# Gated two-branch mixer: skip and spectral rows summed by ScalarE and an accumulating DMA, back rotation finished by an accumulating DMA, new pacing of the two streams

## Chip, cores and metric

One core of a Trainium2 chip (trn2) runs the kernel. The metric is device time in microseconds (us) from the start of the launch to its end. A profiled execution is also cut into a trace, whose span runs from the first to the last instruction.

## The reference

The input `x` has 2048 rows of 1024 values. Two branches are computed from it and mixed row by row:

```
g   = sigmoid(sum(x * gate_w, -1))                      # one gate per row
a   = irfft2(rfft2(x) * (w_r + i w_i))                  # spectral branch
Lb  = exp(dt * Lambda);  Bb = ((Lb - 1) / Lambda) * B   # state-space branch
h_t = Lb * h_(t-1) + Bb @ x_t                           # 1024 complex states
b_t = 2 * Re(C @ h_t) + x_t * Dskip
out = g * a + (1 - g) * b
```

`x * Dskip` is called the skip part here, and `g * a` the gated spectral part. Inputs and output are bf16.

## The kernel before

The work has two streams that share all engines, and an output stage.

**The spectral stream** (`fstage`, then `fft_main`) does the 2-D transform as matrix products: `fstage` folds and transforms along one part of the rows, `fd`, `bf_w` and `bi` (16 groups `g`) do the column transform, the product with the filter and the first inverse step, and `idm` and `fi` (16 indices `j`) the rest. The result `ya` goes to a scratch array in DRAM (L576), 256 KB for each of 16 writes, and is read back by row tiles later.

**The state-space stream** (`ssm_all`) handles the recurrence in 4 chunks `c` of 512 time steps and 4 quarters `q` of the states, 16 blocks in all. Each block has a part on TensorE, `ssm_pe`: 4 groups of 8 matmuls `psu` (L388), and after each group one ScalarE copy with a scale into the tile `u` (L390). The tile `u` has two buffers, and the PSUM tile of a group has two as well. The part on VectorE, `ssm_dve`, rotates the states so that the recurrence becomes real (three operations, L399, L401, L403), scans (L408, four instructions), keeps the carry for the next chunk (L417 to L421), and rotates back: two products (L425, L427) and their sum `h` (L429). `h` is in bf16, 128 partitions of 2 x 2 x 512. The rotation tables of a quarter are made by `tables` in chunk 0. For chunk 1 the tile `h` lies in `big`, for chunk 2 in `xT`, and for chunks 0 and 3 in four tiles of their own.

**The output stage** (from L726) works on 16 row tiles `tb` of 128 rows. A tile belongs to chunk `tb // 4` and has two halves of 512 columns. `half(tb, dh)` runs 16 matmuls `psy` of 512 columns (L770), which read all four `h` tiles of the chunk, two matmuls for each of 8 state blocks. For `tb < 11` the skip part is added by one more matmul, the row tile `xc` (multiplied by `Dskip` on VectorE, L758) with an identity matrix (L774). VectorE then leaves PSUM with one operation (L779): `psy * (1 - g) + gac`, where ScalarE has multiplied the spectral row tile `gac` by the gate (L760). For `tb >= 11` the skip part is taken into an fp32 row tile `xf` by ScalarE (L763) and VectorE (L764) instead. The PSUM tile `psy` has three buffers.

**What sets the order.** The functions are Python generators. `ssm_all` and `fft_main` count their own estimated time `t`, and a loop (L717 to L720) takes the next step from the state-space stream while its `t` lies below a line in the other's `t`: 20 by the spectral stream's 54.4, then to 42 over the next 35. Steps then run up to 43 (L792), and a second loop (L796 to L800) interleaves the rest with the halves of the output stage, with the factor 1.02. A scheduler orders the instructions of an engine from this program order, with its own estimates. SyncE (SP, which issues most DMAs) and GpSimd (POOL) keep the written order up to L748 (`order1`); after that the scheduler orders them too. Semaphores between engines follow from the tiles. The final order of every engine is fixed when the kernel is built.

Of the kernel before, what the change touches and what calls it, by code (L numbers as in the profile page):

```python
# [20 lines left out]
D = 1024  # L21
K = 512
P = 128
# [113 lines left out]
def kernel(  # L137
# [213 lines left out]
    def tables(q):  # L351
        xa = rp.tile([P, 2 * TC], FP32, name="xa", tag="cu")
        for jj in range(2):
            jb = 2 * q + jj
            xj = xa[:, TC * jj:TC * (jj + 1)]
            if q < 2:
                nc.vector.tensor_scalar(out=xj, in0=tau_f, scalar1=thp[:, jb:jb + 1], scalar2=beta[:, jb:jb + 1],
                                        op0=ALU.mult, op1=ALU.add)
            else:
                nc.scalar.activation(out=xj, in_=tau_f, func=ACT.Identity, scale=thp[:, jb:jb + 1],  # L360
                                     bias=beta[:, jb:jb + 1])
        rr, ra = frac(xa, 2 * TC, "xa", rp, "su")
        tq = tab[:, 2 * q:2 * q + 2]
        rr = rr.rearrange("p (a t) -> p a t", a=2)
        ra = ra.rearrange("p (a t) -> p a t", a=2)
        nc.scalar.activation(out=tq[:, :, 0, :], in_=ra, func=ACT.Sin, scale=-TWO_PI_LO, bias=chpi)
        nc.scalar.activation(out=tq[:, :, 1, :], in_=rr, func=ACT.Sin, scale=-TWO_PI_LO)
        nc.vector.tensor_scalar_mul(out=tq[:, :, 2, :], in0=tq[:, :, 1, :], scalar1=-1.0)

# [24 lines left out]
    def ssm_dve(c, q, u):  # L394
# [29 lines left out]
        h = h_tile(c, q)  # L424
        nc.vector.tensor_mul(out=cu, in0=su, in1=tq[:, :, 0:1, ::-1].to_broadcast(full))  # L425
# [4 lines left out]
        hs[c, q] = h  # L430
# [65 lines left out]
    def bf_w(g):  # L496
# [17 lines left out]
        (nc.vector.tensor_copy if g < 3 else nc.scalar.copy)(out=X[:, :, 1:513:2], in_=po)  # L514
# [88 lines left out]
    def fft_main():  # L603
# [24 lines left out]
        for jj in range(9):  # L628
            if jj < 8:
# [8 lines left out]
                if jj == 4:  # L638
                    gt = gates()
                    next(gt)  # L640
                    yield 2.0
                if jj == 4 + 1:
                    next(gt)
                    yield 0.3
# [37 lines left out]
    def ssm_all():  # L682
        prev = iter(())
        for c in range(NCH):
            for q in range(4):
                if c == 0:
                    tables(q)
# [29 lines left out]
    while not fft.done:  # L717
        if ssm.t < (20 * (fft.t - 3.5) / (54.4 - 3.5) if fft.t < 54.4 else 20 + (42 - 20) * (fft.t - 54.4) / 35.0):
            ssm.step()
        else:  # L720
            fft.step()
# [4 lines left out]
    with ExitStack() as bctx:  # L726
# [7 lines left out]
        def load_xc(tb):  # L734
            xcs[tb] = fin.tile([P, D], BF16, name="xc", bufs=3)
            nc.sync.dma_start(out=xcs[tb], in_=x[P * tb:P * (tb + 1), :])

        def load_gac(tb):
            gacs[tb] = fin.tile([P, D], BF16, name="gac", bufs=4)
            nc.sync.dma_start(out=gacs[tb], in_=ya_dram[P * tb:P * (tb + 1), :])  # L740

        for tb in range(3):
            load_xc(tb)
        load_gac(0)
        load_gac(1)
        load_C(1)
        load_gac(2)
        order1.close()  # L748

        psys = {}  # L750

        def half(tb, dh):
# [3 lines left out]
            psy, xc, gac = psys[tb], xcs[tb], gacs[tb]  # L756
            if dh == 0:
                nc.vector.tensor_mul(out=xc, in0=xc, in1=dsk_bc)  # L758
            else:
# [71 lines left out]
```

## Time and profile before

| | us |
|---|---|
| median of 13 runs | 354.85 |
| lowest, highest | 353.06, 358.51 |
| the profiled execution | 358.51 |
| its span in the trace | 356.7 |
| TensorE (PE) busy in the span | 330.8 |
| VectorE (DVE) busy | 302.6 |
| ScalarE (ACT) busy | 178.2 |
| GpSimd (POOL) busy | 28.7 |

The profiled execution is the slowest of the 13. Some 1.8 us of its time lie outside of the span. Its TensorE clock was granted at 0.989 of full speed over the span. The spectral stream ends at about 165 us of the span (the last `ya` write is issued at 165.8 us), and the first `psy` matmul starts at 165.82 us. The busy time of an engine says how full it is, not whether the end waits for it; the chain that ended last and the list of waits are needed for that. A matmul in the trace lasts longer (379 ns) than the distance to the next one, since matmuls overlap.

### The profile page before, as it was taken

Reading aid. Unit: us, or ns where it says so; the run is one execution under the profiler, and the core shown is the slowest. Engines: PE = TensorE matmul, PEld = TensorE weight load, DVE = VectorE, ACT = ScalarE, POOL = GpSimd, SP = SyncE. Lnnn points to the kernel's source line nnn. Section 1 sums busy time; section 2 is a strip of 40 time slices with the busy share of each in tenths; the row PEclk is TensorE's granted clock in tenths of the full one; section 3 lists DMA queues with packets and bytes.
Section 4 is the critical chain, followed back from the end, with each engine's and each line's share of the span. In section 5 each row is a group of like instructions: output and inputs, shape, how many; then the busy total and the mean of one; then the engine's idle time right before and its main releaser. Section 6 shows DMA issues by size and latency. Waiting matters only on the chain.

```text
span 356.7 us, 4881 instructions
## 1 busy us (share of the span) xinstructions
PE 330.8 (93%) x1826; PEld 174.9 (49%) x1826; DVE 302.6 (85%) x423; ACT 178.2 (50%) x245; POOL 28.7 (8%) x73
## 2 busy tenths in 40 slices
PE   2788989999789999989799999999999999999995
PEld 1565656566456565644244444444444444444442
DVE  3998849978988989895949999999999999999441
ACT  1987978779669886984332332313223223223110
POOL 4330421222111000000000000000000000000000
PEclk9999999999989999999899999999999999999999
DMA  7979998989979230214990321211202202142201
GB/s 251 354 96 228 212 243 189 163 205 123 196 163 211 73 118 31 88 59 157 246 188 6 113 88 60 88 29 61 88 4 87 88 0 88 42 138 75 75 29 59
DMA packets 65864, 42.91 MB, mean 120 GB/s; under 512 B 52400, under 2 KB 55472, under 8 KB 65840
## 3 DMA queue, kind: packets, MB, share of 16 engines
q1 hardware_dynamic: 64144, 38.75, 44.0%
q0 software_dynamic: 1344, 3.68, 4.8%
q8 instruction: 14, 0.23, 0.3%
q10 hardware_dynamic: 352, 0.17, 0.2%
q14 instruction: 10, 0.08, 0.1%
HBM read 21.61 MB, written 8.39 MB: 84 GB/s over the span
## 4 chain that ended last, share of the span: by engine, by line
PE 64%; issue 13%; DVE 10%; DMA 8%; POOL 3%; ACT 1%; DVEq 0%; POOLq 0%; SPq 0%; ACTq 0%
PE psy L770 30%; PE psu L388 23%; PE ps_id L550 3%; DMA xt<-in_A_x_dram 3%; DVE su L408 3%; DMA W<-in_A_w_i_dram 3%; POOL W L239 2%; PE psy L774 1%; DMA W<-in_A_w_r_dram 1%; DMA xc<-in_A_x_dram 1%; PE ps_y L569 1%; DVE cu L425 1%; PE ps_y L572 1%; PE ps_q L539 1%; PE ps_y L571 1%
## 5 line engine op out<-in xcount | busy, mean ns | idle before, releaser
L388 PE MATMUL psu<-xT,BT 128*128 128x512 bf16 x512 | 121.0, 380 | 1.4 <-DMA xT<-in_A_x_dram 1.4
L388 PEld LDWEIGHTS <-BT 128*128 128x128 bf16 x512 | 49.7, 98 | 58.2 <-issue 4.0
L408 DVE TENSOR_TENSOR_SCAN su<-r_sb,carry,cu 128x512 bf16<-128x512 f32 x48 | 57.8, 1265 | 0.4
L390 ACT ACTIVATE u<-psu,nrho 128x512 bf16<-128x512 f32 x32 | 22.1, 689 | 59.9 <-PE psu L388 59.9
L770 PEld LDWEIGHTS <-h 128*128 128x128 bf16 x256 | 25.5, 99 | 31.6 <-issue 2.6
L390 ACT ACTIVATE u<-psu,rho 128x512 bf16<-128x512 f32 x32 | 22.3, 696 | 34.4 <-PE psu L388 34.3
L760 ACT ACTIVATE gac<-gac,gf 128x1024 bf16<-128x1024 bf16 x16 | 18.3, 1147 | 29.9 <-DMA gac<-ya_scratch 27.9
L399 DVE TENSOR_TENSOR cu<-u,tab 128x2048 bf16<-128x2048 bf16 x16 | 19.6, 1222 | 15.5 <-ACT u L390 15.4
L770 PE MATMUL psy<-CT,h 128*128 128x512 bf16 x128 | 30.3, 392 | 0.0
L770 PE MATMUL psy<-big,h 128*128 128x512 bf16 x128 | 28.9, 379 | 0.0
L543 ACT CAST big<-ps_q 128x1024 bf16<-128x1024 f32 x16 | 16.6, 1038 | 10.0 <-PE ps_q L542 9.8
L770 PEld LDWEIGHTS <-xT 128*128 128x128 bf16 x128 | 12.5, 98 | 15.1
L770 PEld LDWEIGHTS <-big 128*128 128x128 bf16 x128 | 12.5, 98 | 15.1
L401 DVE TENSOR_TENSOR su<-u,tab 128x2048 bf16<-128x2048 bf16 x16 | 19.7, 1231 | 0.0
L403 DVE TENSOR_TENSOR cu<-cu,su 128x2048 bf16<-128x2048 bf16 x16 | 19.5, 1220 | 0.2
L425 DVE TENSOR_TENSOR cu<-su,tab 128x2048 bf16<-128x2048 bf16 x16 | 19.5, 1220 | 0.1
L481 PE MATMUL ps_d<-G_sb,big 128*128 128x256 bf16 (+3 forms) x128 | 19.6, 294 | 0.0
L539 PE MATMUL ps_q<-MM,Y 128*128 128x256 bf16 x64 | 15.4, 275 | 4.5 <-DVE Y L520 4.3
L427 DVE TENSOR_TENSOR u<-su,tab 128x2048 bf16<-128x2048 bf16 x16 | 19.5, 1220 | 0.0
L465 PE MATMUL ps_f<-BT,eo 128*128 128x256 bf16 x64 | 15.8, 290 | 3.5 <-DVE big L470 2.4
L408 DVE TENSOR_TENSOR_SCAN su<-r_sb,cu 128x512 bf16<-128x512 f32 x16 | 18.9, 1212 | 0.1
L518 DVE TENSOR_TENSOR Y<-X,W 128x1028 bf16<-128x1028 bf16 x16 | 11.1, 692 | 8.3 <-ACT X L514 8.2
(171 smaller groups left out, 548.2 us busy)
## 6 DMA issues: line engine op xcount, KB each, us to landing
ya_scratch<-ya SPq DMA_DIRECT2D x16, 256.0 KB, 2.0
xc<-in_A_x_dram SPq DMA_DIRECT2D x16, 256.0 KB, 2.6
gac<-ya_scratch SPq DMA_DIRECT2D x16, 256.0 KB, 2.7
out_dram<-o SPq DMA_DIRECT2D x15, 256.0 KB, 2.0
MM<-c_MM SPq DMA_DIRECT2D x16, 192.0 KB, 4.2
xt<-in_A_x_dram SPq DMA_DIRECT2D x4, 512.0 KB, 4.8
CT<-in_A_x_dram SPq DMA_DIRECT2D x4, 512.0 KB, 7.7
W<-in_A_w_r_dram POOLq DMA_DIRECT2D x14, 128.2 KB, 3.9
```

The lines of the kernel that those rows point to most:

```text
L388: nc.tensor.matmul(psu, lhsT=BT[:, jb, ri, dblk, :], rhs=xT[:, dblk, TC * c:TC * (c + 1)], start=(dblk == 0), stop=(dblk == 7))
L390: nc.scalar.activation(out=u[:, jj, ri, :], in_=psu, func=ACT.Copy, scale=(nrho if ri else rho)[:, jb:jb + 1])
L399: nc.vector.tensor_mul(out=cu, in0=u, in1=tq[:, :, 0:1, :].to_broadcast(full))
L401: nc.vector.tensor_mul(out=su, in0=u[:, :, ::-1, :], in1=tq[:, :, 1:3, :])
L403: nc.vector.tensor_add(out=cu, in0=cu, in1=su)
L408: nc.vector.tensor_tensor_scan(out=su[:, jj, ri, :], data0=r_sb[:, jb:jb + 1].to_broadcast([P, TC]), data1=cu[:, jj, ri, :], initial=(0.0 ...
L425: nc.vector.tensor_mul(out=cu, in0=su, in1=tq[:, :, 0:1, ::-1].to_broadcast(full))
L427: nc.vector.tensor_mul(out=u, in0=su[:, :, ::-1, :], in1=tq[:, :, 1:3, ::-1])
L481: nc.tensor.matmul(ps[:, lo:lo + w], lhsT=FX[:, q, 8 * g:8 * g + 8, :], rhs=G_sb[:, o:o + w], start=start, stop=stop, skip_group_check=True)
L539: nc.tensor.matmul(dst, lhsT=Yr[:, e:e + 255:2], rhs=ri_, start=True, stop=False, **kw)
L760: nc.scalar.activation(out=gac, in_=gac, func=ACT.Copy, scale=gf[:, tb:tb + 1])
L770: nc.tensor.matmul(psy[:, ds], lhsT=hs[c, jb // 2][:, jb % 2, ri, P * tq:P * (tq + 1)], rhs=CT[dh][:, jb, ri, :], start=(i == 0), stop=(i ...
```

## The change

Five edits are made together.

1. **Output stage.** The identity matmuls are gone, and so is the VectorE addition L764. For every tile, `prep_d` multiplies `xc` by `Dskip` (VectorE), and `prep_a` scales `gac` by the gate (ScalarE), writes `xc * (1 - g)` into an fp32 tile `xf` (ScalarE), and adds `gac` into `xf` by a DMA that accumulates, issued from GpSimd. The last operation on VectorE then reads `psy` and `xf`. `prep_a(n)` also issues the loads of `xc` and `gac` for tile `n + 2`. The buffers of `xc` go from 3 to 2 and those of `gac` from 4 to 3; `xf` has three. Each `prep` call is placed at a tile's end by the list `pre`.
2. **Written order.** ScalarE and SyncE keep the program order from here to the end; the scheduler orders the other engines.
3. **Back rotation.** For chunks 2 and 3, except for the block (3, 3), the first product is written straight to `h`, the second to `cu`, and a DMA from GpSimd adds `cu` to `h`. The VectorE addition is gone for these 7 blocks, and `u` isn't written there.
4. **Pacing.** The line of the first loop goes through 17 (not 20) at 54.4, the steps before the output stage go up to 47 (not 43), the factor of the last loop is 1.08 (not 1.02). The gates are computed one index later (`jj == 5`).
5. **Tables and one copy.** `tables` works on halves of 512 columns instead of 1024, and one more PSUM copy (group 3) goes from ScalarE to VectorE.

```diff
--- before.py
+++ after.py
@@ -350,22 +350,28 @@
 
     def tables(q):
         xa = rp.tile([P, 2 * TC], FP32, name="xa", tag="cu")
+        kk = rp.tile([P, 2 * TC], FP32, name="xa_k", tag="su")
+        tq = tab[:, 2 * q:2 * q + 2]
         for jj in range(2):
             jb = 2 * q + jj
-            xj = xa[:, TC * jj:TC * (jj + 1)]
+            xj, kj = xa[:, TC * jj:TC * (jj + 1)], kk[:, TC * jj:TC * (jj + 1)]
             if q < 2:
                 nc.vector.tensor_scalar(out=xj, in0=tau_f, scalar1=thp[:, jb:jb + 1], scalar2=beta[:, jb:jb + 1],
                                         op0=ALU.mult, op1=ALU.add)
+                yield
             else:
                 nc.scalar.activation(out=xj, in_=tau_f, func=ACT.Identity, scale=thp[:, jb:jb + 1],
                                      bias=beta[:, jb:jb + 1])
-        rr, ra = frac(xa, 2 * TC, "xa", rp, "su")
-        tq = tab[:, 2 * q:2 * q + 2]
-        rr = rr.rearrange("p (a t) -> p a t", a=2)
-        ra = ra.rearrange("p (a t) -> p a t", a=2)
-        nc.scalar.activation(out=tq[:, :, 0, :], in_=ra, func=ACT.Sin, scale=-TWO_PI_LO, bias=chpi)
-        nc.scalar.activation(out=tq[:, :, 1, :], in_=rr, func=ACT.Sin, scale=-TWO_PI_LO)
+            nc.vector.tensor_scalar(out=kj, in0=xj, scalar1=MAGIC, scalar2=-MAGIC, op0=ALU.add, op1=ALU.add)
+            yield
+            nc.vector.tensor_sub(out=xj, in0=xj, in1=kj)
+            nc.vector.tensor_scalar(out=kj.bitcast(I32), in0=xj.bitcast(I32), scalar1=0x7FFFFFFF, scalar2=None,
+                                    op0=ALU.bitwise_and)
+            yield
+            nc.scalar.activation(out=tq[:, jj, 0, :], in_=kj, func=ACT.Sin, scale=-TWO_PI_LO, bias=chpi)
+            nc.scalar.activation(out=tq[:, jj, 1, :], in_=xj, func=ACT.Sin, scale=-TWO_PI_LO)
         nc.vector.tensor_scalar_mul(out=tq[:, :, 2, :], in0=tq[:, :, 1, :], scalar1=-1.0)
+        yield
 
 
     hs = {}
@@ -422,12 +428,19 @@
             carry[q] = cy
         yield
         h = h_tile(c, q)
+        hs[c, q] = h
+        if (c>=2 and (c,q)!=(3,3)):
+            nc.vector.tensor_mul(out=h, in0=su, in1=tq[:, :, 0:1, ::-1].to_broadcast(full))
+            yield
+            nc.vector.tensor_mul(out=cu, in0=su[:, :, ::-1, :], in1=tq[:, :, 1:3, ::-1])
+            nc.gpsimd.dma_start(out=h, in_=cu, accum_op=ALU.add)
+            yield
+            return
         nc.vector.tensor_mul(out=cu, in0=su, in1=tq[:, :, 0:1, ::-1].to_broadcast(full))
         yield
         nc.vector.tensor_mul(out=u, in0=su[:, :, ::-1, :], in1=tq[:, :, 1:3, ::-1])
         yield
         nc.vector.tensor_add(out=h, in0=cu, in1=u)
-        hs[c, q] = h
         yield
 
 
@@ -511,7 +524,7 @@
         nc.tensor.matmul(po[:, 0, :], lhsT=Mi, rhs=OIm, start=False, stop=True)
         nc.tensor.matmul(po[:, 1, :], lhsT=Mn, rhs=ORe, start=True, stop=False)
         nc.tensor.matmul(po[:, 1, :], lhsT=Mr, rhs=OIm, start=False, stop=True)
-        (nc.vector.tensor_copy if g < 3 else nc.scalar.copy)(out=X[:, :, 1:513:2], in_=po)
+        (nc.vector.tensor_copy if g < 4 else nc.scalar.copy)(out=X[:, :, 1:513:2], in_=po)
         W = WT[g]
         Y = fr.tile([P, 2, 514], BF16, name="Y")
         t2 = gc1.tile([P, 2, 514], BF16, name="t2")
@@ -635,11 +648,11 @@
                 nc.vector.tensor_add(out=pm[:, :, 0, :], in0=yp[:, :, 0, :], in1=yp[:, :, 1, :])
                 nc.vector.tensor_sub(out=pm[:, :, 1, :], in0=yp[:, :, 0, :], in1=yp[:, :, 1, :])
                 pms[jj] = pm
-                if jj == 4:
+                if jj == 5:
                     gt = gates()
                     next(gt)
                     yield 2.0
-                if jj == 4 + 1:
+                if jj == 5 + 1:
                     next(gt)
                     yield 0.3
             if jj > 0:
@@ -684,7 +697,8 @@
         for c in range(NCH):
             for q in range(4):
                 if c == 0:
-                    tables(q)
+                    for _ in tables(q):
+                        yield 0.0
                 u = up.tile([P, 2, 2, TC], BF16, name="u", tag="u")
                 for i, _ in enumerate(ssm_pe(c, q, u)):
                     yield 0.5
@@ -715,7 +729,7 @@
     ssm = Gen(ssm_all())
     fft = Gen(fft_main())
     while not fft.done:
-        if ssm.t < (20 * (fft.t - 3.5) / (54.4 - 3.5) if fft.t < 54.4 else 20 + (42 - 20) * (fft.t - 54.4) / 35.0):
+        if ssm.t < (17 * (fft.t - 3.5) / (54.4 - 3.5) if fft.t < 54.4 else 17 + (42 - 17) * (fft.t - 54.4) / 35.0):
             ssm.step()
         else:
             fft.step()
@@ -732,69 +746,77 @@
         xcs, gacs = {}, {}
 
         def load_xc(tb):
-            xcs[tb] = fin.tile([P, D], BF16, name="xc", bufs=3)
+            xcs[tb] = fin.tile([P, D], BF16, name="xc", bufs=2)
             nc.sync.dma_start(out=xcs[tb], in_=x[P * tb:P * (tb + 1), :])
 
         def load_gac(tb):
-            gacs[tb] = fin.tile([P, D], BF16, name="gac", bufs=4)
+            gacs[tb] = fin.tile([P, D], BF16, name="gac", bufs=3)
             nc.sync.dma_start(out=gacs[tb], in_=ya_dram[P * tb:P * (tb + 1), :])
 
-        for tb in range(3):
+        for tb in range(2):
             load_xc(tb)
-        load_gac(0)
-        load_gac(1)
+            load_gac(tb)
         load_C(1)
-        load_gac(2)
         order1.close()
-
-        psys = {}
+        if ('Activation','SP'):
+            bctx.enter_context(tc.manual_schedule(engines=set(getattr(mybir.EngineType, e) for e in ('Activation','SP'))))
+
+        psys, xfs = {}, {}
+
+        def prep_d(tb):
+            nc.vector.tensor_mul(out=xcs[tb], in0=xcs[tb], in1=dsk_bc)
+
+        def prep_a(tb):
+            xc, gac = xcs.pop(tb), gacs.pop(tb)
+            nc.scalar.activation(out=gac, in_=gac, func=ACT.Copy, scale=gf[:, tb:tb + 1])
+            xf = fin.tile([P, D], FP32, name="xf", bufs=3)
+            nc.scalar.activation(out=xf, in_=xc, func=ACT.Copy, scale=om_f[:, tb:tb + 1])
+            nc.gpsimd.dma_start(out=xf, in_=gac, accum_op=ALU.add)
+            xfs[tb] = xf
+            if tb + 2 < 16:
+                load_xc(tb + 2)
+                load_gac(tb + 2)
 
         def half(tb, dh):
             c, tq = tb // 4, tb % 4
             if dh == 0:
                 psys[tb] = psY.tile([P, D], FP32, name="psy", tag="psy")
-            psy, xc, gac = psys[tb], xcs[tb], gacs[tb]
-            if dh == 0:
-                nc.vector.tensor_mul(out=xc, in0=xc, in1=dsk_bc)
-            else:
-                nc.scalar.activation(out=gac, in_=gac, func=ACT.Copy, scale=gf[:, tb:tb + 1])
-                if tb >= 11:
-                    xf = rp.tile([P, D], FP32, name="xf", tag="cu")
-                    nc.scalar.activation(out=xf, in_=xc, func=ACT.Copy, scale=om_f[:, tb:tb + 1])
-                    nc.vector.tensor_add(out=xf, in0=xf, in1=gac)
-                    gac = xf
+            psy = psys[tb]
             ds = slice(512 * dh, 512 * (dh + 1))
             i = 0
             for jb in range(8):
                 for ri in range(2):
                     nc.tensor.matmul(psy[:, ds], lhsT=hs[c, jb // 2][:, jb % 2, ri, P * tq:P * (tq + 1)],
-                                     rhs=CT[dh][:, jb, ri, :], start=(i == 0), stop=(i == 15 and tb >= 11))
+                                     rhs=CT[dh][:, jb, ri, :], start=(i == 0), stop=(i == 15))
                     i += 1
-            if tb < 11:
-                nc.tensor.matmul(psy[:, ds], lhsT=ident, rhs=xc[:, ds], start=False, stop=True)
             if dh == 0:
                 return
             o = fin.tile([P, D], BF16, name="o")
             for ds in ((slice(0, D),) if tb < 15 else (slice(0, 512), slice(512, D))):
-                nc.vector.scalar_tensor_tensor(out=o[:, ds], in0=psy[:, ds], scalar=om_f[:, tb:tb + 1], in1=gac[:, ds],
-                                               op0=ALU.mult, op1=ALU.add)
+                nc.vector.scalar_tensor_tensor(out=o[:, ds], in0=psy[:, ds], scalar=om_f[:, tb:tb + 1],
+                                               in1=xfs[tb][:, ds], op0=ALU.mult, op1=ALU.add)
                 nc.sync.dma_start(out=out2[P * tb:P * (tb + 1), ds], in_=o[:, ds])
 
         def c_all():
             order = [(0, 0), (1, 0), (2, 0), (0, 1), (1, 1), (2, 1)] + [(tb, dh) for tb in range(3, 16) for dh in range(2)]
+            pre = {(0, 0): [(prep_d, 0), (prep_d, 1)], (1, 0): [(prep_a, 0)], (2, 0): [(prep_a, 1)],
+                   (0, 1): [(prep_d, 2)], (1, 1): [(prep_a, 2), (prep_d, 3)], (2, 1): [(prep_a, 3), (prep_d, 4)]}
+            for n in range(4, 16):
+                pre.setdefault((n - 1, 1), []).append((prep_a, n))
+                if n < 15:
+                    pre.setdefault((n - 1, 1), []).append((prep_d, n + 1))
             for tb, dh in order:
-                if dh == 0 and 3 <= tb + 1 < 16:
-                    load_xc(tb + 1)
-                    load_gac(tb + 1)
                 half(tb, dh)
+                for f, n in pre.get((tb, dh), ()):
+                    f(n)
                 yield 3.6
 
-        while ssm.t < 43:
+        while ssm.t < 47:
             ssm.step()
         cg = Gen(c_all())
         t0 = ssm.t
         while not cg.done:
-            if not ssm.done and ssm.t - t0 <= cg.t * 1.02:
+            if not ssm.done and ssm.t - t0 <= cg.t * 1.08:
                 ssm.step()
             else:
                 cg.step()
```

## The prediction

> **What bounds the kernel now.** I read the page's busy shares first, then the chain that ended last in order of time, then busy time by windows of 20 us, then who waited for whom, then the timeline around the start and the end of the output stage.
>
> ```profile
> PE 330.8 (93%) x1826; PEld 174.9 (49%) x1826; DVE 302.6 (85%) x423; ACT 178.2 (50%) x245; POOL 28.7 (8%) x73
> ```
> ```profile
> 173.94 0.38 PE psy L774
> 174.32 1.43 PE psu L388 x5
> 175.75 4.79 PE psy L770 x16
> 180.54 0.22 PE psy L774
> 180.75 3.45 PE psu L388 x16
> 184.21 3.45 PE psy L770 x16
> ...
> 318.02 34.55 PE psy L770 x160
> 352.60 0.75 DVE o L779
> ```
> The chain (start, us, what) is TensorE without a hole from 173.94 to 352.60. A row of 16 takes 3.45 us, so one matmul costs 0.2158 us, and each L774 entry is an identity matmul standing on that chain.
>
> ```profile
> 80.00:100.00 20.00, 16.39 (x116) 10.17 (x114) 18.06 (x28) 15.03 (x21) 3.72 (x6) 1.00 1.00 159
> ...
> 220.00:240.00 20.00, 20.00 (x95) 9.05 (x93) 19.83 (x24) 4.83 (x7) 0.00 (x0) 1.00 0.18 53
> 240.00:260.00 20.00, 20.00 (x94) 9.04 (x93) 19.86 (x21) 6.38 (x9) 0.00 (x0) 1.00 0.20 66
> ```
> Columns: window, length, then PE, PE's loads, DVE, ACT, POOL busy with counts, clock, DMA share, GB/s. In the output stage TensorE and VectorE are both full; in the spectral stage (first row) neither is.
>
> ```profile
> 324.77 3.62 PE L770 MATMUL psy<-CT,h 128*128 128x512 bf16 x16
> 325.37 1.22 DVE L429 TENSOR_TENSOR h<-cu,u 128x2048 bf16<-128x2048 bf16 x1
> ```
> The last h, block (3,3), is done at 326.6. Tile 12 starts at 324.77 and reads it with its 13th matmul, at 324.77 + 12 x 0.2158 = 327.4. VectorE is thus only 0.8 us from being the bound. Taking the identity matmuls away alone would gain next to nothing. This is the central point: both engines must get lighter by about the same amount.
>
> ```profile
> PE psy L774 <- DVE xc L758: 2.1, 1, 2.1
> DVE cu L399 <- ACT u L390: 15.4, 10, 4.5
> ```
> The first identity matmul also holds TensorE for 2.1 us, as its xc comes late.
>
> **What the Trainium skill says.** (1) "DMA: Bandwidth & Descriptors", SWDGE vs HWDGE vs iDMA: accumulation during a DMA is only for DMAs issued from GpSimd, so every such addition goes through POOL's queue. (2) Same page, Anatomy of one DMA, SWDGE path: about 2.0 us + bytes / 436e3. The trace's only such transfers, the filter loads (128 KB, L239), landed in 3.9 us at the median and 9.4 at most, in a stage where the DMA engines are full. (3) Same page, Issuing engines are not separate DMA queues: all share 16 engines and interleave. (4) "SBUF — State Buffer", Who interferes with whom: VectorE operations in a 2-port mode block GpSimd's descriptor writing; tensor_tensor doesn't. The trace agrees as far as it goes: POOL's issue took 536 to 624 ns except one of 1018, with VectorE 90% busy, and L518 beside it stayed at 672 to 698 ns.
>
> **The change, part by part.** I count matmuls in the order of the built kernels, from the first psy (call it T). Before: 512 psy + 312 psu + 22 identity = 846, x 0.2158 = 182.6 us, plus the stall of 2.1. After: 512 + 296 = 808, 174.4 us. The 16 psu that are missing now stand ahead of T (pacing to 47), 3.45 us. So TensorE saves 22 x 0.2158 = 4.75, and 2.1 for the stall: 6.9 us, if it stays dense.
>
> VectorE must follow. From the timeline, starts lie 1.14 us apart for a 2048-wide operation, 1.19 for a scan, 1.2 for L779, 0.6 for an xc product; the carry takes 0.25. A block before costs 6 x 1.14 + 4 x 1.19 + 0.25 + 0.6 + 1.2 = 13.65 with its tile's share, and TensorE gave it one per 66 matmuls, 14.24. I add these up in VectorE's order, each operation no earlier than its input; for before this puts the last h at T + 156.9. With T = 165.8 and 3.7 for the stall and a slow row of 16 matmuls after it, that is 326.4; the trace has 326.6, so the ledger may be trusted.
>
> After, chunk 2 and 3 blocks cost 12.5, since L429 is gone 7 times (8.0 us) and one L764 ahead of the end (1.1). TensorE now gives one per 64 matmuls, 13.8. The ledger has VectorE 9 us behind at T + 38, when chunk 1 is done, and h(3,3) at T + 144.0. Tile 12's 13th matmul comes at T + 146.7 + 2.6 = 149.3 (the last psu now ends 24 us ahead of tile 12, not 14). Spare: 5.3 us, where there was 0.8.
>
> What may eat this spare is SP's written order. Load xc(n+2) now stands behind the store of tile n-1, and VectorE's product for it stands two operations (2.28 us) behind L779 of that tile. The store's issue takes 0.43, then
>
> ```profile
> 327.96 0.33 SPq L736 DMA_DIRECT2D xc<-in_A_x_dram  x1
> 331.10 0.69 DVE L758 TENSOR_TENSOR xc<-xc,dsk_bc 128x1024 bf16<-128x1024 bf16 x1 [0.27 <-DMA xc<-in_A_x_dram]
> ```
> 3.1 us from issue to use; the median landing is 2.6. Call the sum d, from L779's end to use: 3.05 to 3.7. Each of six blocks (xc 5 to 10) waits d - 2.28. The ledger had d = 3.05; at 3.7 h(3,3) comes at 147.9, still in time. Limit: d = 3.98. The accumulating DMA of the block is in flight just then; for all of 512 KB it may add up to 1.4 us to d.
>
> The accumulating DMAs: 16 of 256 KB and 7 of 512 KB. Priced as copies, 2.6 and 3.2 us (estimate from the page); upper bound the 9.4 us seen under load. I take 4. Nobody waits closely: POOL's order puts each xf DMA a whole block (13 us) ahead of its L779; a cu comes free two blocks later; h(3,2), written at T + 129, is read at 148. In the tail, tile 13 has the least: xc at 151, xf near 153, needed at 162. A DMA of 9 us still fits. POOL's issue (about 0.6 each) is on a queue with nothing else; its first four xf issues stand ahead of the first h, 60 us before that is read.
>
> ScalarE in written order: 16 x (1.15 + 1.15) us. What is queued behind a waiting prep_a is the next copy of psu into u, and then TensorE, with two PSUM tiles. xf(n) waits for an xc product made about a tile before, and 3.45 us of psy cover its 2.3 us: nothing. If that cover is gone, up to 2.3 us for a tile. The tightest place I find is u's buffer at T + 37, needed by 39. SP's move of both loads ahead of the transposes costs 0.8 us there; CT's second half is first used at T + 22, after the transposes' end near T + 14: nothing.
>
> Tables and L514: VectorE gains 12 short operations (about 0.06 each) and one copy (0.74), ScalarE 8 halves of Sin (fixed part about 0.2 each, 1.6) less a copy (0.77). Pacing leaves 14 fewer psu done by group 12 (73 against 87) and the same number at the spectral stream's end (176). TensorE has holes there (16.39 of 20), so I take zero, between -2 and +2. Gates later: zero, the same work.
>
> Sum: span 356.7 - 6.9 = 349.8, and with 1.8 around it 351.6 against the profiled 358.51. That execution is the slowest of 13; taken off their median, 354.85 - 6.9 = 348.0.
>
> **Rivals.**
> A (50%): TensorE stays dense from T on, 348.0; with the spectral stage's bounds 346 to 350.
> B (22%): d between 4.0 and 5.1, as the accumulating DMA slows the xc load. At 4.4, h(3,3) is at 152.1, TensorE waits 2.8: 350.8; range 348.5 to 353.5. For it: DMA engines shared. Against: their share in this stage is 0.2.
> C (10%), slower: the same place, with the full price. It decides from d = 5.2, where six waits of 2.9 eat the gain; at d = 5.8, h(3,3) comes at 160.5, 11.2 late: 359. It needs loads twice as slow as those shown.
> D (10%): the spectral stage also gains, since less VectorE work stands before its Y (TensorE waited 4.3 us for L520): 345.
> E (8%): the change only shifts the waits, e.g. ScalarE's order holds psu by 0.7 us a block for ten blocks: 355.
>
> Faster: A + B nearly whole + D, 0.80. Within 0.3% (about what a measurement of this kernel can tell from no change): E, 0.08. Slower: C and a spectral stage made worse, 0.12. The range is D's end to B's end.
>
> **What would show it.** Right: L774's 22 matmuls gone, psy and psu dense from T on, T near 169, 174 us from T to the last psy. L429 nine, and VectorE idle near tile 12. Accumulating DMAs landing in 3 to 5 us. xc products (now L767) waiting for their DMA 0.7 to 1.4 us six times. Wrong: PE waiting for L443 at tile 12 (B, C), ACT's copies of psu late behind xf (E), or T far from 169 (D, or its opposite).

## The result and the profile after

| | before | after |
|---|---|---|
| median, us | 354.93 | 370.43 (367.71 to 374.26) |
| ratio, 95% interval | | 1.041 [1.038, 1.044] |
| span of the profiled execution | 356.7 | 371.5 |
| T, start of the first `psy` | 165.82 | 172.82 |
| from T to the end of the last `psy` | 186.7 | 193.3 |

The change makes the kernel 4.1% slower; the forecast was 348.0 us, faster. The profiled execution of the kernel after took 373.27 us, a disturbed run above its median, so its parts are read to about a microsecond.

The first view is the page's busy times of the kernel after (share of the span, instructions).

```profile
PE 328.0 (88%) x1804; PEld 173.9 (47%) x1804; DVE 289.4 (78%) x424; ACT 189.5 (51%) x263; POOL 49.7 (13%) x96
```

TensorE and VectorE both did less than before (330.8 and 302.6 us), as forecast, and yet the span grew by 15 us. So the time went into waiting. The windows of 20 us of the kernel after (columns as in the prediction) show where it begins.

```profile
220.00:240.00 20.00, 20.00 (x95) 9.07 (x93) 15.41 (x19) 7.57 (x10) 3.16 (x3) 1.00 0.42 93
240.00:260.00 20.00, 20.00 (x94) 9.02 (x93) 14.81 (x16) 7.38 (x10) 2.42 (x3) 1.00 0.42 88
260.00:280.00 20.00, 20.00 (x94) 9.11 (x93) 12.68 (x14) 5.62 (x8) 2.18 (x2) 1.00 0.59 125
...
320.00:340.00 20.00, 10.19 (x40) 4.24 (x40) 19.32 (x17) 2.19 (x2) 3.17 (x4) 0.74 0.54 132
```

VectorE, full before (19.8 of 20), now has 13 to 15 of 20. TensorE stays full while VectorE falls behind, waits for the first time at 292, 70 us after the start of this table, and loses half of the window 320 to 340. The DMA share doubled, from 0.2 to 0.42 and more. A table of busy shares taken from 220 to 280 would have called VectorE relieved; it was late.

The chain that ended last was TensorE alone in this stage before. In the kernel after it reads (start, us, what):

```profile
240.33 6.31 DMA xc<-in_A_x_dram
246.66 0.69 DVE xc L767
247.35 1.15 DVE cu L409
248.52 4.82 DVE su L414 x4
...
254.81 1.14 DVE cu L435
255.95 1.21 DVE o L796
257.17 0.34 SPq L798
257.60 6.04 DMA xc<-in_A_x_dram
263.67 0.69 DVE xc L767
```

From 240 to 307 the chain is a ring: a block on VectorE ends with L796, its store is issued by SyncE, behind it the next `xc` load, and VectorE waits for that load before it goes on with the next block. One turn takes 17.0 us (246.66 to 263.67), where TensorE gives a block every 13.8. The timeline of the kernel after shows one such wait (start, duration, engine; idle time and its releaser in brackets).

```profile
255.87 1.28 DVE L796 SCALAR_TENSOR_TENSOR o<-psy,om_f,xf 128x1024 bf16<-128x1024 f32 x1
256.50 1.26 POOL L436 DMA_DIRECT2D xT<-cu  x1 [16.25 <-DVE cu L435]
257.06 1.22 DVE L405 TENSOR_TENSOR cu<-u,tab 128x2048 bf16<-128x2048 bf16 x1
257.17 0.34 SPq L798 DMA_DIRECT2D out_dram<-o  x1
257.26 1.41 POOL L774 DMA_DIRECT2D xf<-gac  x1
257.60 0.38 SPq L750 DMA_DIRECT2D xc<-in_A_x_dram  x1
258.19 1.22 DVE L407 TENSOR_TENSOR su<-u,tab 128x2048 bf16<-128x2048 bf16 x1
263.67 0.69 DVE L767 TENSOR_TENSOR xc<-xc,dsk_bc 128x1024 bf16<-128x1024 bf16 x1 [4.26 <-DMA xc<-in_A_x_dram]
```

Two accumulating DMAs are issued just ahead of the load, L436 by 1.1 us and L774 by 0.3. The load is used 6.07 us after its issue (before: 3.1), and d, from L796's end to the use, is 6.5. The loads of the six waiting blocks are used 5.4 to 8.0 us after their issue.

One block earlier the DMA of `xf` is not near. There the accumulation of `h` alone stands ahead of the load, and the load is as late, 6.33 us from issue to use.

```profile
238.97 1.28 POOL L436 DMA_DIRECT2D xT<-cu  x1 [11.96 <-DVE cu L435]
...
240.33 0.38 SPq L750 DMA_DIRECT2D xc<-in_A_x_dram  x1
...
246.66 0.69 DVE L767 TENSOR_TENSOR xc<-xc,dsk_bc 128x1024 bf16<-128x1024 bf16 x1 [4.52 <-DMA xc<-in_A_x_dram]
```

The page's DMA issues of the kernel after (count, KB, median us to landing) and the list of waits (sum, times, longest) give the whole; the median landing of `xc` takes in the loads of the start and the tail.

```profile
xf<-gac POOLq DMA_DIRECT2D x16, 512.0 KB, 5.2
...
xc<-in_A_x_dram SPq DMA_DIRECT2D x16, 256.0 KB, 4.8
```
```profile
DVE xc L767 <- DMA xc<-in_A_x_dram: 40.6, 10, 6.1
PE psy L789 <- DVE o L796: 13.0, 2, 12.6
```

Last, TensorE's stall in the timeline of the kernel after.

```profile
328.10 1.28 DVE L796 SCALAR_TENSOR_TENSOR o<-psy,om_f,xf 128x1024 bf16<-128x1024 f32 x1
329.43 5.08 PE L789 MATMUL psy<-CT,xT 128*128 128x512 bf16 x16 [12.65 <-DVE o L796]
338.21 1.22 DVE L443 TENSOR_TENSOR h<-cu,u 128x2048 bf16<-128x2048 bf16 x1
338.35 3.61 PE L789 MATMUL psy<-CT,h 128*128 128x512 bf16 x16 [0.38 <-DVE o L796]
```

The halves of tile 11 need a `psy` buffer. The one they get was filled by tile 8 and is emptied by an L796 (328.10) that stands behind VectorE's late blocks. So TensorE waits 12.65 us for a buffer, one tile ahead of where the last `h` (L443) would have stopped it.

### The profile page after: what moved, and what is told of

It is laid out like the page before. It is cut to its first block, busy times and chain, and to the rows that moved or that the text cites. A ratio compares the mean times of both kernels' runs of the same rounds, so it can differ in the third digit from the quotient of the medians.

```text
span 371.5 us, 4925 instructions
## 1 busy us (share of the span) xinstructions
PE 328.0 (88%) x1804; PEld 173.9 (47%) x1804; DVE 289.4 (78%) x424; ACT 189.5 (51%) x263; POOL 49.7 (13%) x96
## 3 DMA queue, kind: packets, MB, share of 16 engines
q0 software_dynamic: 6192, 15.74, 20.5%
## 4 chain that ended last, share of the span: by engine, by line
DVE 30%; PE 30%; issue 17%; DMA 15%; SPq 3%; POOL 2%; ACT 2%; DVEq 0%; POOLq 0%; ACTq 0%
PE psu L394 14%; DVE su L414 10%; PE psy L789 8%; DMA xc<-in_A_x_dram 7%; DMA MM<-c_MM 3%; DMA xt<-in_A_x_dram 3%; DVE cu L409 3%; SPq L216 2%; DVE o L796 1%; POOL xf L774 1%; PE ps_d L494 1%; DVE t L532 1%; DVE cu L405 1%; DVE cu L435 1%; DMA xT<-in_A_x_dram 1%
## 5 line engine op out<-in xcount | busy, mean ns | idle before, releaser
L767 DVE TENSOR_TENSOR xc<-xc,dsk_bc 128x1024 bf16<-128x1024 bf16 x16 | 10.9, 689 | 40.6 <-DMA xc<-in_A_x_dram 40.6
L774 POOL DMA_DIRECT2D xf<-gac x16 | 15.8, 1026 | 133.6 <-PE psu L394 75.6
L789 PE MATMUL psy<-CT,h 128*128 128x512 bf16 x128 | 28.9, 379 | 0.4 <-DVE o L796 0.4
L789 PE MATMUL psy<-CT,xT 128*128 128x512 bf16 x64 | 15.9, 406 | 12.6 <-DVE o L796 12.6
L796 DVE SCALAR_TENSOR_TENSOR o<-psy,om_f,xf 128x1024 bf16<-128x1024 f32 (+1 forms) x17 | 20.6, 1215 | 6.0 <-DMA xf<-gac 6.0
L789 PEld LDWEIGHTS <-big 128*128 128x128 bf16 x128 | 12.5, 98 | 15.1
L494 PE MATMUL ps_d<-G_sb,big 128*128 128x256 bf16 (+3 forms) x128 | 18.8, 286 | 0.0
```

Source lines behind the costliest of these rows:

```text
L494: nc.tensor.matmul(ps[:, lo:lo + w], lhsT=FX[:, q, 8 * g:8 * g + 8, :], rhs=G_sb[:, o:o + w], start=start, stop=stop, skip_group_check=True)
L774: nc.gpsimd.dma_start(out=xf, in_=gac, accum_op=ALU.add)
L789: nc.tensor.matmul(psy[:, ds], lhsT=hs[c, jb // 2][:, jb % 2, ri, P * tq:P * (tq + 1)], rhs=CT[dh][:, jb, ri, :], start=(i == 0), stop=(i ...
L796: nc.vector.scalar_tensor_tensor(out=o[:, ds], in0=psy[:, ds], scalar=om_f[:, tb:tb + 1], in1=xfs[tb][:, ds], op0=ALU.mult, op1=ALU.add)
```

## The experiments

The theory after the result: the cause is where VectorE's `xc` product stands. It comes two operations behind the L796 whose store precedes the load on SyncE, with two `xc` buffers; every us of d beyond 2.28 stops the whole VectorE stream. The accumulating DMAs only make the load long enough to matter. Three rivals: the accumulating DMAs are too slow in themselves, and taking them out is the remedy; the new pacing costs the time; the tables in halves cost it.

The start of the middle part, the first `idm` matmul, wandered between 108 and 113 us in runs whose code is the same up to there. So for the part before T the table below gives the time from the first `idm` to the last `fi` matmul, and for the part after it T to the last `psy`. "Block waits" is the sum of VectorE's waits for `xc` before the last `h`. All kernels are changes of the kernel after, but for k11, a change of the one before. Each ratio is to the kernel before as it was measured beside that kernel, with medians from 354.93 to 355.88 us. "xc landing" is the page's median over the loads whose landing the trace shows, start and tail included.

| kernel | median, us | ratio to before | first idm to last fi | T to last psy | xc landing | block waits |
|---|---|---|---|---|---|---|
| before | 354.93 | | 50.0 | 186.7 | 2.6 | 0 |
| after | 370.43 | 1.041 [1.038, 1.044] | 53.8 | 193.3 | 4.8 | 27.4 |
| k1: edit 3 undone | 359.43 | 1.010 [1.004, 1.016] | 53.7 | 180.6 | 3.1 | 5.9 |
| k2: loads a tile earlier | 367.42 | 1.032 [1.027, 1.038] | 53.7 | 191.0 | 5.0 | 24.2 |
| k3: h's DMA plain | 362.93 | 1.022 [1.016, 1.027] | 53.7 | 183.8 | 4.2 | 17.9 |
| k4: first loop's pacing undone | 365.48 | 1.027 [1.024, 1.031] | 50.6 | 191.3 | 4.9 | 25.5 |
| k6: k1 and k4 | 356.00 | 1.004 [1.002, 1.007] | 50.6 | 181.4 | 3.4 | 6.8 |
| k10: product into its own tile | 351.66 | 0.992 [0.989, 0.995] | 53.8 | 174.6 | 4.6 | 0 |
| k10p: k10 and k4 | 347.58 | 0.979 [0.977, 0.982] | 50.6 | 174.6 | 3.9 | 0 |
| k11: before, with edit 3 | 357.15 | 1.005 [1.003, 1.008] | 50.0 | 186.8 | 2.7 | 0 |
| k12: k10p, edit 5 undone | 346.89 | 0.976 [0.973, 0.979] | 50.0 | 174.6 | 4.0 | 0 |
| k13: k10p, later pacing undone | 348.17 | 0.979 [0.976, 0.982] | 50.6 | 178.0 | 2.7 | 1.1 |
| k14: k10p, edit 3 undone | 348.16 | 0.981 [0.978, 0.984] | 50.6 | 175.2 | 2.7 | 0 |

**k1, the rotation's sum back on VectorE.**

```
-        if (c>=2 and (c,q)!=(3,3)):
+        if False:
```

> The changed kernel with one part undone: the back rotation's sum is again a VectorE addition in all 16 blocks, so the 7 accumulating DMAs of h (512 KB each) are gone; the 16 accumulating DMAs of xf stay, and so does SyncE's written order. Theory 1 (the xc load stands behind the store in SyncE's order, and it lands late because the accumulating DMA of h is in flight just then): xc lands again in about 3 us, VectorE's waits for it fall from 40 us to under 10, the last h comes about 3 us late, and the median is about 355 us (15 us below the changed kernel) although VectorE has 8 us more work. Rival (written order alone makes the load late, whatever else is in flight): waits stay near 4 us a block, the 8 us of additions come on top, and the time is 370 us or more.

11 us come back, so these DMAs matter. But the kernel is still 1% slower than before, and 4 us slower than expected: VectorE got its 7 sums again (8.0 us), and waits for `xc` remain, 20.5 us in all where under 10 were expected. The list of waits of k1 (engine, line, what it waited for: sum, times, longest):

```profile
DVE xc L767 <- DMA xc<-in_A_x_dram: 20.5, 9, 5.5
...
PE psu L394 <- ACT u L396: 5.2, 5, 1.9
```

Of these, 5.9 us lie before the last `h`: the product still stands two operations behind L796, and the load, shorter now (3.1), holds it 0.8 to 1.8 us in five blocks. The DMA of `xf` moved too: in these blocks it is issued 4 to 6 us behind the load, so k1 doesn't tell the two kinds of accumulation apart. TensorE stops where `psu` needs a copy into `u`, five times, behind the late blocks. Taking the DMAs out of the rotation is thus not the whole remedy.

**k2, the loads a tile earlier.**

```
-            xcs[tb] = fin.tile([P, D], BF16, name="xc", bufs=2)
+            xcs[tb] = fin.tile([P, D], BF16, name="xc", bufs=3)
...
-            gacs[tb] = fin.tile([P, D], BF16, name="gac", bufs=3)
+            gacs[tb] = fin.tile([P, D], BF16, name="gac", bufs=4)
...
-        for tb in range(2):
+        for tb in range(3):
...
-            xf = fin.tile([P, D], FP32, name="xf", bufs=3)
+            xf = fin.tile([P, D], FP32, name="xf", bufs=2)
...
-            if tb + 2 < 16:
-                load_xc(tb + 2)
-                load_gac(tb + 2)
+            if tb + 3 < 16:
+                load_xc(tb + 3)
+                load_gac(tb + 3)
```

> The changed kernel with xc and gac loaded one tile earlier (three tiles ahead; xc 3 buffers, gac 4, xf 2 instead of 3), with all accumulating DMAs kept. Theory 1: VectorE no longer waits for xc in blocks 9 to 14, the last h is done near T + 140, TensorE is dense to the end, and the median is about 351 us. Rival (the accumulating DMAs slow the output stage by themselves, through h or xf arriving late): the xc waits go, but TensorE or VectorE waits for h or xf instead, and the time stays above 362 us.

The block waits stayed: 3.6 to 4.5 us, six times. In the built order the scheduler had moved the product a tile earlier as well. `xc(7)`'s product now stands two operations behind L796 of tile 3, where it stood behind that of tile 4, and its load still follows that tile's store. The run was meant to give the load time and did not. Its time lies in the rival's range, but the waits for `xc` that the rival saw gone are still there, so it decides nothing. What it shows is that a buffer gives slack only if the use doesn't move up with it.

**k3, a plain copy in place of the accumulation.** Here `h` is overwritten by the second product and the first is left out; all else stays, POOL's issue included.

```
-            nc.gpsimd.dma_start(out=h, in_=cu, accum_op=ALU.add)
+            nc.gpsimd.dma_start(out=h, in_=cu)
```

> The changed kernel with the DMA of cu to h a plain copy instead of an accumulation (the first product of the back rotation is overwritten, so that part of the sum is left out); same bytes of source, same queue, same order. If the reading and rewriting of the destination is what keeps the DMA engines busy, xc lands in 3 to 4 us and the median is 352 to 357 us. If any 512 KB transfer beside the load does it, xc still lands in 5 to 6 us and the time stays near 370 us.

Both kernels' L436 in the trace, the kernel after first (duration of the issue in ns, then the time to landing, lowest, median, highest), then k3:

```profile
L436 POOL DMA_DIRECT2D xT<-cu x4: 1264/1278/1280, 221.7 to 273.5; - x4
...
DMA to landing us min/median/max: 4.6/7.4/8.2
```
```profile
L436 POOL DMA_DIRECT2D xT<-cu x4: 767/784/790, 218.6 to 263.6; - x4
...
DMA to landing us min/median/max: 2.9/3.4/4.2
```

The accumulating kind takes over twice as long as the copy of the same bytes. With the copy the first four block waits fall from 4.3 to 4.5 us to 2.0 to 2.4, while the last two are 4.5 each (3.6 and 6.1 in the kernel after). In all, 9.5 of the 27.4 us go, and the time lies between both expected ranges. The last two blocks show why: there the copy lands in 2.9 us, but the accumulation of `xf` is issued 0.5 us ahead of the load, which is used 6.3 us after its issue.

```profile
295.61 0.55 POOL L436 DMA_DIRECT2D h<-cu  x1 [15.58 <-DVE cu L435]
296.14 0.90 POOL L774 DMA_DIRECT2D xf<-gac  x1
...
296.71 0.59 SPq L750 DMA_DIRECT2D xc<-in_A_x_dram  x1
302.97 0.69 DVE L767 TENSOR_TENSOR xc<-xc,dsk_bc 128x1024 bf16<-128x1024 bf16 x1 [4.45 <-DMA xc<-in_A_x_dram]
```

In the first two blocks of k3, with the copy of `h` alone ahead, the load is used 4.0 and 3.8 us after its issue, for 6.3 with the accumulation. In the two blocks between, where the DMA of `xf` is issued only 0.3 us ahead, it is 4.2. So the accumulation of `h` alone is enough to make the load this late, and so is that of `xf` beside a plain copy, if it is half a microsecond ahead.

**k4, the first loop's pacing undone.**

```
-                if jj == 5:
+                if jj == 4:
...
-        if ssm.t < (17 * ... else 17 + (42 - 17) * (fft.t - 54.4) / 35.0):
+        if ssm.t < (20 * ... else 20 + (42 - 20) * (fft.t - 54.4) / 35.0):
```

> The changed kernel with the pacing of the spectral stage put back (20 at 54.4, gates one index earlier); the output stage is unchanged. Theory 1: the first psy comes at 169 us instead of 173, as TensorE no longer waits for pm and lrow, and the whole is 3 to 4 us faster, about 367 us. Rival (the tables in halves, or chance, made the first psy late): it stays at 173 us and the time at 370 us.

The middle part takes 50.6 us in place of 53.8, near the kernel before (50.0), while T to the last `psy` falls by 1.9 us, as much as the block waits do (25.5 for 27.4). The median falls by 5 us, where 3 to 4 were expected. The rival of the pacing holds for 3.2 us, and ahead of T only. **k6** undoes both parts:

> The changed kernel with the back rotation's sum on VectorE in all blocks and the pacing of the spectral stage put back: what remains is the output stage by ScalarE and the accumulating DMA of xf, the written orders, the later start and the tables. Both theories: 3 us less than with the rotation on VectorE alone (359.4), 356 us, level with the kernel before: what the 22 identity matmuls gave, VectorE's lateness takes.

As expected, it returns to the time of the kernel before, within half a per cent, and its waits are those of k1 again.

**k10, the product into a tile of its own.** This is the run that decides. All 23 accumulating DMAs stay, and so does the pacing. The product goes to a new tile, so the `xc` buffer is free as soon as the product is made, and `prep_d` issues the loads there. In the built order a load still follows a store, but one tile earlier: xc(8) follows the store of tile 4, where xc(7) did.

```
-            nc.vector.tensor_mul(out=xcs[tb], in0=xcs[tb], in1=dsk_bc)
+            xms[tb] = fin.tile([P, D], BF16, name="xm", bufs=1)
+            nc.vector.tensor_mul(out=xms[tb], in0=xcs.pop(tb), in1=dsk_bc)
+            if tb + 2 < 16:
+                load_xc(tb + 2)
+                load_gac(tb + 2)
...
-            xf = fin.tile([P, D], FP32, name="xf", bufs=3)
+            xf = fin.tile([P, D], FP32, name="xf", bufs=2)
...
-            if tb + 2 < 16:
-                load_xc(tb + 2)
-                load_gac(tb + 2)
```

> The changed kernel with the product of xc with Dskip written to a tile of its own (one buffer; xf 2 buffers instead of 3), so that the load of xc may start a tile earlier and the product stands two tiles behind it on VectorE. All 23 accumulating DMAs, their bytes and the written order of SyncE and ScalarE stay. Theory 1 (the loss is VectorE's wait for xc, the DMAs only make it long): the loads still land in 4 to 6 us, but VectorE's waits for xc fall below 8 us in sum, TensorE is dense after the first psy (175 to 178 us to the last), and the median is 350 to 354 us. Rival (the accumulating DMAs harm in another way too, as xf or h come late): the sum of other waits rises and the time stays above 362 us.

The page and the timeline of k10:

```profile
xc<-in_A_x_dram SPq DMA_DIRECT2D x16, 256.0 KB, 4.6
```
```profile
245.27 0.68 DVE L768 TENSOR_TENSOR xm<-xc,dsk_bc 128x1024 bf16<-128x1024 bf16 x1
...
245.89 1.28 POOL L436 DMA_DIRECT2D xT<-cu  x1 [10.88 <-DVE cu L435]
246.65 1.43 POOL L778 DMA_DIRECT2D xf<-gac  x1
...
247.60 0.39 SPq L750 DMA_DIRECT2D xc<-in_A_x_dram  x1
...
258.05 0.68 DVE L768 TENSOR_TENSOR xm<-xc,dsk_bc 128x1024 bf16<-128x1024 bf16 x1
...
270.61 0.68 DVE L768 TENSOR_TENSOR xm<-xc,dsk_bc 128x1024 bf16<-128x1024 bf16 x1
```

Both accumulating DMAs still stand just ahead of the load, and the loads land as late as in the kernel after, 4.6 us at the median and up to 8.0. VectorE doesn't wait for one of them: the load issued at 247.60 is used at 270.61, 23 us later. A block takes 12.78 us (245.27 to 258.05), not 17.0, and T to the last `psy` is 174.6; the median, 351.66 us, is in the expected range. The DMAs' slowness is thus harmless here, where the load has more than a block's lead, and they need not go: the first rival falls. k10 moves the load, the tile and the product's place together, so it doesn't tell which of the three was needed.

**k10p, k10 and the old pacing.**

> The same, and the pacing of the spectral stage put back as before (20 at 54.4, gates one index earlier). Theory 1 adds the two: some 3 us less than with the product's own tile alone, 347 to 350 us, which is faster than both kernels. Rival (the pacing and the late output stage are not additive, since an earlier first psy finds VectorE further behind): no gain over the product's own tile alone.

The median is 347.58 us, within the expected range: the two gains add up. Windows of k10p, to set against those of the kernel after:

```profile
220.00:240.00 20.00, 19.89 (x93) 9.07 (x93) 19.79 (x23) 7.31 (x10) 2.15 (x2) 1.00 0.59 116
240.00:260.00 20.00, 19.89 (x92) 9.02 (x93) 19.83 (x23) 5.73 (x8) 4.36 (x4) 1.00 0.61 129
260.00:280.00 20.00, 19.89 (x92) 9.11 (x93) 19.86 (x18) 8.06 (x10) 1.72 (x2) 1.00 0.63 152
```

VectorE is full again, TensorE too, at a DMA share of 0.6, higher than in the slower kernel. So what the DMA engines carried was not the limit.

**k11, the kernel before with edit 3 only**, the same seven blocks' sums by the accumulating DMA.

> The kernel before with one part of the change alone: the back rotation's sum in 7 blocks by an accumulating DMA from GpSimd. Theory 1: VectorE gets 8 us lighter but TensorE was dense already, so nothing is gained; the xc loads slow to 5 us, and the products, which wait three tiles behind, hold VectorE by a few us that the lighter load covers: 354 to 357 us. Rival (an accumulating DMA of h beside the loads costs as much here as in the changed kernel): 362 us or more.

7.9 us of VectorE's busy time are gone (294.7 for 302.6) and the kernel is 0.5% slower, at the upper end of what was expected: TensorE was dense already, and still waits 2.1 us for the first `xc`, and 1.5 us for the last `h`. One part of the expectation failed: the `xc` loads were to slow to 5 us, and they land in 2.7, although the accumulations into `xT` take 7.2. One block of k11:

```profile
246.77 0.33 SPq L744 DMA_DIRECT2D xc<-in_A_x_dram  x1
247.07 1.26 POOL L430 DMA_DIRECT2D xT<-cu  x1 [12.93 <-PE psy L782]
```

The load and the accumulation start in the same microsecond here too, but in six of the seven blocks the load is issued 0.1 to 0.3 us ahead of the accumulation, and in the first 1.7, not 1.1 to 1.4 us behind it as in the kernel after. The `gac` loads, issued 1.1 to 1.7 us behind it, do slow down, to 4.8 us at the median from 2.7 in the kernel before. So in these traces it is the load issued behind the accumulating DMA that lands late, and not the one issued ahead of it. The store ahead of the load is not enough for that: in k1 it stands there too, and the load is used 2.6 to 3.6 us after its issue.

**k12 to k14, parts of the change taken out of k10p.** k12 has the tables in one piece and the copy back on ScalarE (edit 5 undone), k13 the later pacing (43 and 1.02), k14 the rotation's sum on VectorE. Of k12 the code of the tables is left out here.

```
k12: ...
     -(nc.vector.tensor_copy if g < 4 else nc.scalar.copy)(out=X[:, :, 1:513:2], in_=po)
     +(nc.vector.tensor_copy if g < 3 else nc.scalar.copy)(out=X[:, :, 1:513:2], in_=po)
k13: -        while ssm.t < 47:
     +        while ssm.t < 43:
     -            if not ssm.done and ssm.t - t0 <= cg.t * 1.08:
     +            if not ssm.done and ssm.t - t0 <= cg.t * 1.02:
k14: -        if (c>=2 and (c,q)!=(3,3)):
     +        if False:
```

> The best version with the rotation tables in pieces of 1024 columns and the group 3 copy on ScalarE, as before. Prediction's value for that edit: zero, so 347 to 348.5 us. If the smaller pieces free the spectral groups earlier (VectorE serves them in between), 349 us or more; if their fixed parts cost, below 346.5 us.

> The best version with the output stage's start and interleaving of before (43 and 1.02 instead of 47 and 1.08). The ledger puts the last h at T + 151.5 and its deadline at T + 152.8, so TensorE should just stay dense: the same time, 347 to 349 us. Rival (the spare between the last psu and tile 12 is needed): TensorE waits at tile 12 by 2 us or more, 350 us or more.

> The best version (product in its own tile, pacing of before) with the back rotation's sum on VectorE again, so no accumulating DMA of h. Theory 1, by the ledger: VectorE has no waits for xc, but 8 us more work, and the last h comes at T + 147 where the deadline is T + 149: it just holds, 347 to 349 us, so the back rotation's DMA is worth at most 1 us once the xc waits are gone. Rival (both engines had to get lighter by about the same amount): without it TensorE waits at tile 12, and the time is 351 us or more.

All three lie within 0.7 us of k10p, with overlapping intervals. k13 and k14 came out as expected, and k12 a tenth of a microsecond below its range for no effect. The third rival is bounded by k12: the halves and the copy cost 0.7 us by the medians, and 0.6 from the first `idm` to the last `fi`. k13's 178.0 holds 16 `psu` more behind T, 3.45 us, which its T has less. k12, at 346.89 us the fastest, beats the kernel before by 2.4% [2.1, 2.7]. The written order (edit 2) was not undone by itself in any kernel.

## Why the prediction was wrong

**The time, by its own sum.** For the profiled execution the prediction's parts were T 169.3 and, from there to the last `psy`, 186.7 - 6.9 - 3.45 = 176.35. Measured: T 172.82, which is 3.5 more; 193.3, which is 17.0 more; and from the last `psy` to the end 5.4 in place of 4.1, as the last L796 waited 4.86 us for its `xf` DMA. Together some 21.7 us, the difference of 373.27 and the forecast 351.6.

**The step that failed** is "Call the sum d, from L779's end to use: 3.05 to 3.7", with "for all of 512 KB it may add up to 1.4 us to d". The place was right, and so were the count of six waits and their price of d - 2.28. The size was not: d measured 6.8, 6.8, 6.5, 6.7, 5.8 and 8.4. The waits sum to 27.4 us, where the ledger at d = 3.05 had 4.6. Put into that ledger they give the last `h` at T + 144.0 + 22.8 = T + 166.8; the trace has 338.21 + 1.22 - 172.82 = T + 166.6. So the ledger held to 0.2 us with the right d. It also holds without waits: it gives T + 139.4 for k10, and the trace has T + 139.4; for k13 it gave T + 151.5, as in the trace. What misled was "Against: their share in this stage is 0.2". That was the share of the kernel before, and the change itself brought the transfers that raised it to 0.42 to 0.59. The Trainium skill's page "DMA: Bandwidth & Descriptors" (Issuing engines are not separate DMA queues), which the prediction cites, says that the queues share 16 engines and interleave; this case puts a number to it: the same load was used 3.1 us after its issue before, and 5.4 to 8.0 us behind the accumulating DMAs. The prediction saw that such a DMA would be in flight, and priced it at 1.4 us at most. k3 and k11 show that the delay comes from the transfers issued just ahead of the load, and k10 that it hurts only where the product stands close behind.

**Rival C**, slower through d above 5.2, was the mechanism, at 10%. It "needs loads twice as slow as those shown"; in the six blocks they took 6.4 us from issue to use on average, twice the 3.1 shown. Its price at d = 5.8 was 359; at the measured mean of 6.8 the same sum gives 365. Its other half, TensorE waiting for the last `h` at tile 12, came out in another place: tile 11's first half, for a `psy` buffer. The prediction followed `h` alone and not L796, which VectorE executes in the same late stream.

**How lateness turns into time.** By the ledger, block waits and added VectorE work together may reach 4.6 + 5.3 = 9.9 us before TensorE stops: the 4.6 us of waits that it held already, and its spare. Set against T to the last `psy` beyond the dense 174.5:

| | waits + added work | beyond 9.9 | T to last psy beyond 174.5 |
|---|---|---|---|
| k10 | 0 | 0 | 0.1 |
| k14 | 0 + 8.0 | 0 | 0.7 |
| k1 | 5.9 + 8.0 | 4.0 | 6.1 |
| k6 | 6.8 + 8.0 | 4.9 | 6.9 |
| k3 | 17.9 | 8.0 | 9.3 |
| k2 | 24.2 | 14.3 | 16.5 |
| k4 | 25.5 | 15.6 | 16.8 |
| after | 27.4 | 17.5 | 18.8 |

One threshold and one sum order all eight kernels. The six late ones lie 1.2 to 2.2 us above it. In the kernel after, 15.1 us of the 18.8 are TensorE's three waits (12.65, 2.10, 0.38); nearly all of the other 3.7 is in the 16 matmuls behind each of the first two waits, which took 5.1 and 4.9 us, not 3.45, in windows with a lower granted clock (0.91 from 280 to 300, 0.74 from 320 to 340).

**TensorE's saving was right.** "TensorE stays dense from T on", 174.4 us: k10, k10p and k12 have 174.6. So the gain was there and was lost to a wait. That k10p with 347.58 meets the forecast 348.0 is partly chance. The forecast's sum has 176.35 from T to the last `psy`, not the 174.4 of its own count: it took off the stall of 2.1 us, but not the slow 16 matmuls behind it, though its ledger has 3.7 for both. These 1.8 us came on top; against them stand 0.6 us for the tables and the spread of the runs. And k10p has the first loop's pacing of before, which the forecast's kernel had not.

**The spectral stage** was taken as "zero, between -2 and +2". It cost 3.8 us (53.8 for 50.0), outside of the bound. k4 gives 3.2 of it back by the first loop's pacing and the gates alone, and k12 the other 0.6 by the tables and the copy; k10 to k10p gives 4.1 in the median. The prediction counted `psu` by group 12 and at the end of the stream, and did not ask what stands between `idm` and `fi`, where TensorE waits for VectorE (2.9 us for `pm`, 1.3 for the gates' row in the kernel after). That the postponed `psu` fall there is my reading; the line and the gates' place were not run apart.

**"Both engines must get lighter by about the same amount"** was too strong. k14 has the identity matmuls gone and the VectorE sums back, and takes 348.16 us. With no waits the ledger gives its last `h` at T + 144.0 - 4.6 + 8.0 = 147.4, and the trace has T + 147.9, still ahead of 149.3. In the kernel before VectorE waited for a copy into `u` five times from T on (0.4 to 4.5 us), which fits: it followed TensorE, and its last `h` moved up when TensorE got lighter. The seven DMAs are worth 0.6 us here, with overlapping intervals. Taken alone (k11) they are worth nothing.

**Smaller steps.** The limit d = 3.98 is 3.93 by the prediction's own numbers (144.0 + 6 x 0.88 = 149.3), which changes nothing. "I take 4" us for the accumulating DMAs: `h` took 7.4, `xf` 5.2. That nobody waits for them closely was right, except for 6.0 us in the tail, 4.86 of them for the last tile. "POOL's issue (about 0.6 each)" was 0.84 to 1.28 us for `h` and 1.0 for `xf`; whether that cost anything was not tried. ScalarE in written order (rival E) held TensorE once in the kernel after, 2.1 us, behind the late stream and not as its cause, since in k10 the same order costs TensorE nothing.

## What to carry to other kernels

A load's time from the profile before holds for the traffic before. Where a change adds transfers, list which will be issued just ahead of the load, within a microsecond or two; in this case that made it twice as long. An engine that consumes a load in a fixed order, right behind the step that lets it start, pays every us of it on everything queued behind. Give the load more lead, and look in the built order whether the use has moved up with it. When following lateness, follow every result of the late engine, its emptying of PSUM buffers too, and not only the one that the forecast was about.

## What the hardware showed unexpectedly

An accumulating DMA of 512 KB within SBUF landed in 7.4 us (4.6 to 8.2), the plain copy of the same tiles in 3.4 (2.9 to 4.2). Its issue on GpSimd took 1.28 us in place of 0.78 for `xT`, and 0.84 in place of 0.55 for the `h` tiles. A load of 256 KB issued 0.1 to 0.3 us ahead of such a DMA landed in 2.5 to 3.8 us (k11); issued 1.1 to 1.4 us behind it, as in the kernel after, it was used 5.4 to 8.0 us after its issue.

Behind its stall of 12.65 us TensorE needed 4.9 us for 16 matmuls that otherwise take 3.45, and the granted clock of that window was 0.74; in the full windows without a stall it was 1.00. From T on, nine waits of TensorE in all the traces were 2.1 us or longer, and behind eight of them 16 matmuls took 4.9 to 5.9 us; behind waits of up to 1.9 us they took 3.7 at most. The runs show that the two come together, not why.
